# A gated attention and expert mix on one core: the spread of reciprocals, the layout of logit operands, a relu and the planner's clock are changed

## The chip, the cores and the metric

The kernel runs on one core of a Trainium2 chip. The metric is the device time of one execution in microseconds (us), smaller is better. Five engines work beside each other, each through its own list of instructions in order: PE (matrix products into the PSUM banks), DVE (vector work), ACT (activations), POOL (general vector work), and SP, which here issues every transfer. Transfers run on 16 DMA engines.

## The reference

A sequence of 2048 tokens of width 640 goes through an attention with 32 heads of width 20, in 4 segments of 512 tokens, with a memory carried from segment to segment. Beside it one token, the one with the largest router score, goes through a feed-forward expert. A gate mixes the two.

```python
phi = lambda t: where(t > 0, t + 1.0, exp(t))
for s in range(4):                                   # segments of 512 tokens
    logits = einsum("bhqd,bhkd->bhqk", qs, ks) * scale + mask
    a_dot  = softmax(logits) @ vs
    a_mem  = (phi(qs) @ M) / (phi(qs) . z + 1e-6)
    o      = g * a_mem + (1 - g) * a_dot             # g: sigmoid(beta), one per head
    M, z   = M + phi(ks)^T vs, z + sum(phi(ks))
a = concat(o) @ wo
b = x, plus sigmoid(r) * SwiGLU(x[i]) at the token i with the largest r = x @ w_r
out = sigmoid(x . gate_w) * a + (1 - sigmoid(x . gate_w)) * b
```

## The kernel before

The work is cut into 8 units (2 halves of 16 heads x 4 segments) and each unit into 4 groups of 4 heads, 32 groups in all; a group is numbered n, its unit u, its place in the unit g, its segment s.

For each unit PE makes the projections (`t_job` for q and k, transposed, in five tiles of 128 rows; `v_job` for v), in three products of split halves (a value is kept as a high part hi and a rest lo, made by `split`: ACT casts, DVE or POOL subtracts). Both run in `paired`, which uses the two row halves of PE at once. A product tile is evacuated by `evac_t`: DVE copies PSUM to `xs`, hi and lo are stored to DRAM by `place`, and phi is made as POOL min with 0 (L671), ACT exp (L672), DVE max (L673). A tile holds pieces of several groups (`TILES`), so `place` stores each piece by itself into an array of its group and kind, `stk`: three blocks of 80 rows, hi, hi, lo for q and hi, lo, hi for k.

For each group `fetch` loads q and k from these arrays as 60 rows x 2 halves x 2 column pairs. `a_step` (six per group) makes logits once only for their row maxima, which DVE takes (L785); `maxima` turns them, and two small transfers add them to q as rows (`qs<-mr`). `b_step` (six) makes the logits again with the maxima subtracted, ACT takes exp (L826), POOL sets the masked half to 0 (L828). `pv_step` multiplies with v, whose extra column of ones gives the sums; DVE copies the result to `pvs` (L851). For s > 0 `memory_read` makes the memory's part `num` and its denominators.

`norm` then divides. The denominators of the four heads, one row each, are collected (`zr<-pvs`, and `zr<-num` before it) into 128 x 16, inverted and gated on DVE, stored to DRAM as rows (`zrow<-zr`), and read back spread over all head rows, `rb<-zrow`: four blocks, each repeated 32 times, 2 KB a row for s = 0 and 4 KB for s > 0. DVE multiplies `pvs` (L872), POOL `num` (L875), DVE adds (L876), and the result goes to `oT` in DRAM, from which `o_load` and `o_job` make the output rows.

The order is written by a planner while the kernel is built. `Plan.add` notes every instruction with a duration, a key (about the number of the group at which it is due) and its buffers; `Plan.order` then plays the engines forward: each engine takes, of the instructions that could start earliest, the one with the lowest key. The transfer clock, the durations (`acts`, `dves`, `pools`) and the keys set the order in which each engine finds its instructions; on the chip that order is fixed, and an engine whose next instruction must wait, waits. All transfers stand in SP's list (`dma`, L376). The lines of the transfer clock before:

```python
count, size = t.desc
busy = max(count * (0.008 + size / 23400.0) / 16.0, 0.03)
dma_free = max(dma_free, t.fin + 0.9) + busy
t.fin = dma_free + 0.9
```

`t.fin` ahead of these lines is the end of the issue, 0.42 us (`ISSUE`) after its start.

Of the kernel before, what the change touches and what calls it, by code (L numbers as in the profile page):

```python
# [9 lines left out]
F32 = mybir.dt.float32  # L10
# [40 lines left out]
LEAD = 3.2  # L51
KPARTS = tuple((g, c0) for rows in TILES for _, _, kind, g, c0 in rows if kind == "k")
# [51 lines left out]
class Plan:  # L104
# [3 lines left out]
    ISSUE = 0.42  # L108
# [64 lines left out]
    def order(self):  # L173
# [22 lines left out]
        def choose(e):  # L196
# [50 lines left out]

        while len(done) < total:
# [85 lines left out]
def tile_infini_mod(  # L334
# [40 lines left out]
    def dma(key, dst, src, reads, writes, desc):  # L375
        plan.add("SP", Plan.ISSUE, lambda: nc.sync.dma_start(dst, src), key, reads, writes, desc=desc)  # L376

# [12 lines left out]
    def acts(n):  # L390
        return 0.2 + n / 1250.0
# [4 lines left out]
    def pools(n):  # L396
        return 0.12 + n / 460.0
# [4 lines left out]
    def split(key, engine, hi, lo, src, n, reads, hpart, lpart):  # L402

        act(key, acts(n), lambda: nc.scalar.copy(hi, src), reads, [hpart])  # L404
        e, dur = (nc.gpsimd, pools(n)) if engine == "POOL" else (nc.vector, dves(n))
        plan.add(engine, dur, lambda: e.tensor_tensor(out=lo, in0=src, in1=f32(hi), op=OP.subtract), key,  # L406
                 [*reads, hpart], [lpart])
# [52 lines left out]
    def constants():  # L460
# [10 lines left out]
        for i in range(4):  # L471
            pool(-4.6 + 0.1 * i, 1.2, lambda t=k_ring.tiles[i]: nc.gpsimd.memset(f32(t), 1.0), [], [kones[i]])
        for i in range(2):
            pool(-4.0, 0.2, lambda t=mneg[i].t: nc.gpsimd.memset(f32(t), 0.0), [], [(mneg[i], p) for p in "zhl"])
# [93 lines left out]
    def paired(ps, steps, operands, n, key_of, reads_of, kind):  # L568

        total, last, phase = len(steps), None, steps[0][1]  # L570
        for i, (k, ph) in enumerate(steps):
# [17 lines left out]
            last = pe(key_of(i), 3 * stream(n) + 0.01, fn, reads_of(k), [ps], opens=ps if i == 0 else None, fence=fence)  # L589
# [65 lines left out]
    def evac_t(u, j, ps, b, key):  # L655
# [11 lines left out]
        for r0, r1, kind, g, c0 in TILES[j]:  # L667
            place(kind, 4 * u + g, c0, hi, lo, r0, r1 - r0, key)
        if s < SEG - 1 or (s > 0 and j != 2):
            e = phi_ring.take()  # L670
            pool(key + 0.2, pools(L), lambda: nc.gpsimd.tensor_scalar(e.t, xs.t, 0.0, None, op0=OP.min), [xs], [e])  # L671
            act(key + 0.2, acts(L), lambda: nc.scalar.activation(e.t, e.t, AF.Exp), [e], [e])  # L672
# [25 lines left out]
    def memory_read(u, g, key):  # L698
# [13 lines left out]
        dma(key, z.t[:, 1, :], rows4(nb.t), [nb], [(z, 1)], (128, 64))  # L712
        pool(key, 0.15, lambda: nc.gpsimd.tensor_scalar(z.t[:, 1, :], z.t[:, 1, :], 1e-6, None, op0=OP.add), [(z, 1)], [(z, 1)])
# [47 lines left out]
    def a_step(n, p, t, key):  # L761
# [22 lines left out]
        for i, at_, w in blocks:  # L784
            dve(key - 0.6, 0.09 + 2 * w / 960.0, lambda i=i, at_=at_, w=w: nc.vector.tensor_reduce(  # L785
                out=m_.t[:, :, p, i], in_=banks[ps.pair][:, :, at_:at_ + w], axis=AX.X, op=OP.max), [ps], [(m_, (p, i))])

    def maxima(n, key):
# [65 lines left out]
    def norm(n, o, key):  # L854
# [17 lines left out]
        dve(key, dves(L), lambda: nc.vector.tensor_tensor(out=o.t, in0=o.t, in1=rb.t[:, 0, :], op=OP.mult), [o, rb], [o])  # L872
        if s:
            nb = nums.pop(n)
            pool(key, pools(L), lambda: nc.gpsimd.tensor_tensor(out=nb.t, in0=nb.t, in1=rb.t[:, 1, :], op=OP.mult), [nb, rb], [nb])  # L875
            dve(key, dves(L), lambda: nc.vector.tensor_tensor(out=o.t, in0=o.t, in1=nb.t, op=OP.add), [o, nb], [o])  # L876
# [26 lines left out]
    def route():  # L903
# [28 lines left out]
        plan.add("SP", 1.2, load, key, [ix], [xr], desc=(128, 20))  # L932
# [96 lines left out]
    def o_load(s, k, key):  # L1029
# [3 lines left out]
        while r < 128:  # L1033
# [11 lines left out]
            dma(key - 0.5, b.t[r:r + cnt, :L], src, [oTb[n] for n in reads], [(b, r)], (cnt, 2048))  # L1045
# [3 lines left out]
    def o_job(s, t, key, span):  # L1049
# [5 lines left out]
        act(key - 0.2, acts(D), lambda: nc.scalar.activation(xf, xf, AF.Copy, scale=R["gb"].t[:, i:i + 1]), [xb, R["gb"]], [xb])  # L1055
        dve(key - 0.2, dves(D), lambda: nc.vector.scalar_tensor_tensor(
# [10 lines left out]
        dve(key + span, dves(D), lambda: nc.vector.scalar_tensor_tensor(  # L1067
# [109 lines left out]
```

## Time and profile before

| | |
|---|---|
| time, median of 3 runs | 918.67 us (915.0 to 923.78) |
| profiled execution: its own time | 923.43 us |
| profiled execution: span, first to last instruction | 921.7 us |
| mean granted clock of PE | 0.841 |
| busy: PE, DVE, ACT, POOL | 654.5, 438.8, 309.8, 370.2 us |
| transfers on SP's queue | 77296 packets, 133.89 MB, 50.4% of the 16 engines' span |

The profile is of one execution. A group of instructions is one source line on one engine with its tiles (out<-in), with the number of instructions, their busy time, the mean of one in ns, and the idle time of the engine just before them with what ended it. The chain is the work that ended last, followed back from the end. In the timeline each row has start, duration, engine, line, tiles, and in brackets the idle time before it. In the table of stretches each row has the stretch, its length, the busy times of PE, PE's weight loads, DVE, ACT and POOL, then PE's granted clock, the share of the DMA engines in use, and GB/s.

### The profile page before, as it was taken

The page shows a single profiled execution, that of the slowest core. Times are in us where ns is not written, and L with a number is a line of the kernel's source. Part 1 is how long each engine was busy: PE and PEld are TensorE (multiplying, and loading weights), DVE is VectorE, ACT ScalarE, POOL GpSimd, SP SyncE. Part 2 cuts the span into 40 slices and gives each one's busy share as a digit, 9 for nine tenths or more (in the row PEclk, how much of TensorE's full clock was granted, in tenths as well). Part 3 has the DMA queues.
Part 4 walks back from the last instruction along what each step waited for, and adds up shares of the span by engine and source line. Part 5 has one row for each costly group of instructions (what it writes and reads, how often), then busy time and mean ns, then how long its engine had stood idle before and what let it go on. Part 6 is the DMA issues. An engine that isn't in the chain of part 4 may idle for free.

```text
span 921.7 us, 19377 instructions
## 1 busy us (share of the span) xinstructions
PE 654.5 (71%) x7760; PEld 486.4 (53%) x7760; DVE 438.8 (48%) x771; ACT 309.8 (34%) x536; POOL 370.2 (40%) x446
## 2 busy tenths in 40 slices
PE   5778778766788763675778679756775956568667
PEld 3675566445545541354556466544444734356567
DVE  8537445643544554444356345533563544443323
ACT  5234345233333342531424325322332324133210
POOL 8735325443433542363334325442443426151310
PEclk9889899779779975876989879977888977779879
DMA  7754562445325544256437664666446753334531
GB/s 232 217 158 127 142 195 85 135 140 154 90 83 158 160 107 118 77 159 196 137 101 208 170 182 126 202 176 176 126 130 187 229 140 128 116 113 137 146 129 73
DMA packets 77386, 135.12 MB, mean 147 GB/s; under 512 B 24338, under 2 KB 27952, under 8 KB 77296
## 3 DMA queue, kind: packets, MB, share of 16 engines
q1 hardware_dynamic: 77296, 133.89, 50.4%
q8 instruction: 61, 1.00, 0.5%
q14 instruction: 29, 0.24, 0.1%
HBM read 87.30 MB, written 45.56 MB: 144 GB/s over the span
## 4 chain that ended last, share of the span: by engine, by line
DMA 39%; PE 27%; DVE 11%; issue 9%; SPq 6%; POOL 5%; ACT 3%; ACTq 0%; POOLq 0%; DVEq 0%
DMA rb<-zrow 15%; PE bank L587 14%; DMA zrow<-zr 6%; SPq L376 6%; PE bank L847 4%; DVE mx L785 3%; DMA qs<-mr 3%; PE bank L821 2%; DMA zr<-pvs 2%; PE bank L773 2%; DMA raw<-in_wc_dram 2%; POOL num L875 2%; DMA out_dram<-xf 2%; PE bank L706 1%; DMA xf<-in_x_dram 1%
## 5 line engine op out<-in xcount | busy, mean ns | idle before, releaser
L785 DVE TENSOR_REDUCE mx<-bank 128x2 f32<-128x1024 f32 (+3 forms) x256 | 199.6, 816 | 54.8 <-PE bank L779 44.9
L773 PE MATMUL bank<-ks,qs 60*128 60x512 f32 (+3 forms) x512 | 93.0, 398 | 64.5 <-DVE mx L785 34.2
L587 PE MATMUL bank<-xhi,whi 64*128 64x512 f32 (+1 forms) x480 | 102.6, 407 | 33.9 <-ACT whi L404 22.9
L875 POOL TENSOR_TENSOR num<-num,rb 128x512 f32<-128x512 f32 x24 | 42.4, 1766 | 170.4 <-DMA rb<-zrow 170.4
L826 ACT ACTIVATE pb<-bank 128x768 f32<-128x768 f32 x128 | 101.1, 816 | 28.2 <-PE bank L821 22.8
L826 ACT ACTIVATE pa<-bank 128x1024 f32<-128x1024 f32 x64 | 65.7, 1027 | 126.9 <-PE bank L821 120.1
L872 DVE TENSOR_TENSOR pvs<-pvs,rb 128x512 f32<-128x512 f32 x32 | 24.3, 758 | 174.1 <-DMA rb<-zrow 174.1
L821 PE MATMUL bank<-qs,ks 62*128 62x512 f32 (+3 forms) x512 | 81.5, 366 | 34.8 <-DMA qs<-mr 19.2
L773 PEld LDWEIGHTS bank<-ks,qs 60*128 60x128 f32 x512 | 54.7, 214 | 83.2 <-DVE mx L785 39.6
L587 PE MATMUL bank<-xhi,wlo 64*128 64x512 f32 (+1 forms) x480 | 96.0, 381 | 3.4 <-DVE wlo L406 2.2
L587 PE MATMUL bank<-xlo,whi 64*128 64x512 f32 (+1 forms) x480 | 95.2, 378 | 0.5 <-POOL xlo L406 0.3
L828 POOL TENSOR_SCALAR_AFFINE_SELECT pb<-pb 128x256 f32<-128x256 f32 (+1 forms) x128 | 73.9, 584 | 42.5 <-ACT pb L826 40.0
L828 POOL TENSOR_SCALAR_AFFINE_SELECT pa<-pa 128x256 f32<-128x256 f32 x64 | 29.6, 463 | 140.6 <-ACT pa L826 139.2
L821 PEld LDWEIGHTS bank<-qs,ks 62*128 62x128 f32 x512 | 51.8, 199 | 54.8 <-issue 10.8
L406 POOL TENSOR_TENSOR xlo<-raw,xhi 128x512 fp32r<-128x512 f32 x53 | 68.4, 1308 | 22.9 <-ACT xhi L404 22.3
L587 PEld LDWEIGHTS bank<-xhi,whi 64*128 64x128 f32 x480 | 53.5, 205 | 44.1 <-ACT whi L404 23.1
L587 PE MATMUL bank<-whi,xhi 64*128 64x320 f32 x320 | 54.8, 338 | 23.0 <-DVE nil L575 19.1
L587 PE MATMUL bank<-vhi,xhi 64*128 64x322 f32 x320 | 64.5, 375 | 6.1 <-DVE nil L575 6.1
L671 POOL TENSOR_SCALAR phi<-xs 128x512 f32<-128x512 f32 x38 | 57.0, 1499 | 23.7 <-DVE xs L664 11.0
L709 ACT COPY num<-bank 128x512 f32<-128x512 f32 x24 | 14.1, 585 | 155.5 <-DVE pvs L851 42.8
L847 PE MATMUL bank<-pb,va 128*32 128x128 f32 (+2 forms) x768 | 56.7, 422 | 5.8 <-POOL pb L828 5.8
L587 PE MATMUL bank<-vlo,xhi 64*128 64x322 f32 x320 | 58.8, 341 | 0.0
(126 smaller groups left out, 1346.8 us busy)
## 6 DMA issues: line engine op xcount, KB each, us to landing
qs<-stkq SPq DMA_DIRECT2D x64, 240.0 KB
ks<-stkk SPq DMA_DIRECT2D x64, 240.0 KB
rb<-zrow SPq DMA_DIRECT2D x24, 512.0 KB
stkq<-hi SPq DMA_DIRECT2D x32, 320.0 KB
raw<-in_xT_dram SPq DMA_DIRECT2D x35, 256.0 KB
oT<-pvs SPq DMA_DIRECT2D x32, 256.0 KB
stkq<-lo SPq DMA_DIRECT2D x32, 160.0 KB
raw<-in_wg_dram SPq DMA_DIRECT2D x15, 288.0 KB
```

The costliest lines, as they stand in the source:

```text
L376: plan.add("SP", Plan.ISSUE, lambda: nc.sync.dma_start(dst, src), key, reads, writes, desc=desc)
L406: plan.add(engine, dur, lambda: e.tensor_tensor(out=lo, in0=src, in1=f32(hi), op=OP.subtract), key, [*reads, hpart], [lpart])
L587: nc.tensor.matmul(t[:, b, :n], w[64 * r:64 * r + 64], m[64 * r:64 * r + 64], start=i == 0 and p == 0, stop=ends and p == 2, skip_group_ch ...
L671: pool(key + 0.2, pools(L), lambda: nc.gpsimd.tensor_scalar(e.t, xs.t, 0.0, None, op0=OP.min), [xs], [e])
L773: nc.tensor.matmul(a[:, b, at_:at_ + w], q.t[64 * b:64 * b + ST, p, 128 * i:128 * i + 128], k.t[64 * b:64 * b + ST, p, :w], start=m == 0, ...
L785: dve(key - 0.6, 0.09 + 2 * w / 960.0, lambda i=i, at_=at_, w=w: nc.vector.tensor_reduce(out=m_.t[:, :, p, i], in_=banks[ps.pair][:, :, at ...
L821: nc.tensor.matmul(bt[:, b, at_:at_ + w], k.t[64 * b:64 * b + ST + 2, p, 128 * c:128 * c + 128], q.t[64 * b:64 * b + ST + 2, p, L - w:], s ...
L826: act(key - 0.4, 0.22 + 2 * w / 1270.0, lambda: nc.scalar.activation(pt.t, banks[ps.pair][:, :, :w], AF.Exp, scale=SCALE), [ps], [pt])
L828: pool(key, 0.42 if t < 2 else 0.64, lambda: nc.gpsimd.affine_select(out=d, in_=d, pattern=[[0, 2], [0, len(cs)], [1, 128]], base=0, chann ...
L847: nc.tensor.matmul(o[32 * j:32 * j + 32, ps.bank, L - w:], v.t[:, c, VW * h:VW * h + 32], pt[j % 2, min(c, 2)].t[:, j // 2, at_:at_ + w], ...
L872: dve(key, dves(L), lambda: nc.vector.tensor_tensor(out=o.t, in0=o.t, in1=rb.t[:, 0, :], op=OP.mult), [o, rb], [o])
L875: pool(key, pools(L), lambda: nc.gpsimd.tensor_tensor(out=nb.t, in0=nb.t, in1=rb.t[:, 1, :], op=OP.mult), [nb, rb], [nb])
```

## The change

- `norm`: the spread of reciprocals is read in four transfers of 20 rows, one per head, in place of one of 128 rows. The 12 rows between heads are set to 1 once, by two memsets on POOL at the start.
- `stk` is one array per unit, three blocks of 640 rows (hi, hi, lo). `place` stores a whole tile: hi twice in one transfer, lo in another. `fetch` picks 20 rows from each of the three blocks, q from the first on, k from the last back, and waits for the tiles that hold its rows.
- phi: POOL's min with 0 goes. ACT makes relu(-x), then exp of its negative; DVE's part stays.
- The transfer clock: 0.65 us from issue to the first byte, packets on as many engines as the transfer is said to use (`wide`: 16, or 10 for `fetch` and the spread), 0.3 us to the end. `ISSUE` is 0.36, with durations of their own for several transfers; several durations of engine work are changed.
- PE's choice: the keys of projection steps are 1.2 later. A step that opens a bank for `a_step` (read by DVE) or `b_step` (read by ACT) loses rank when the work already waiting for that engine reaches more than 0.5 us past the step's end.

```diff
+LATER = 1.2
+PATIENCE = 0.5
+SHY = 2.0
+DRAIN = {"a": "DVE", "b": "ACT"}
+ROWS = {(kind, g): (min(128 * j + r0 for j, rows in enumerate(TILES) for r0, _, k_, g_, _ in rows if (k_, g_) == (kind, g)),
+                    [j for j, rows in enumerate(TILES) for _, _, k_, g_, _ in rows if (k_, g_) == (kind, g)])
+        for kind in "qk" for g in range(4)}
...
-    ISSUE = 0.42
+    ISSUE = 0.36
...
+                late = {}
+                for x in ("ACT", "DVE"):
+                    late[x] = free[x] + sum(t.dur for t in avail[x] if not t.gone)
+
+                def rank(c):
+                    est, t = c
+                    k = t.key
+                    if t.opens is not None and t.opens.kind in DRAIN:
+                        x = late[DRAIN[t.opens.kind]] - (est + t.dur + 0.3) - PATIENCE
+                        if x > 0:
+                            k += SHY * x
+                    return k, t.seq
+                return min(now, key=rank)
...
-                count, size = t.desc
-                busy = max(count * (0.008 + size / 23400.0) / 16.0, 0.03)
-                dma_free = max(dma_free, t.fin + 0.9) + busy
-                t.fin = dma_free + 0.9
+                count, size, wide = t.desc
+                each = 0.008 + size / 23400.0
+                begin = max(dma_free, t.fin + 0.65)
+                dma_free = begin + count * each / 16.0
+                t.fin = max(dma_free, begin + -(-count // wide) * each) + 0.3
...
     def pools(n):
-        return 0.12 + n / 460.0
+        return 0.17 + n / 455.0
...
-    stk = {kind: [Buf(dram.tile([3 * GC, L], F32, name=f"stk{kind}{n}")) for n in range(NG)] for kind in "qk"}
+    stk = [Buf(dram.tile([3 * D, L], F32, name=f"stk{u}")) for u in range(NU)]
...
+        for i in range(2):
+            pool(-1.0, 1.0, lambda t=rb_ring.tiles[i]: nc.gpsimd.memset(t, 1.0), [], [rones[i]])
...
-            last = pe(key_of(i), 3 * stream(n) + 0.01, fn, reads_of(k), [ps], opens=ps if i == 0 else None, fence=fence)
+            last = pe(key_of(i) + (LATER if kind != "O" else 0.0), 3 * stream(n) + 0.01, fn, reads_of(k), [ps], opens=ps if i == 0 else None, fence=fence)
...
-    def place(kind, n, c0, hi, lo, r0, cnt, key):
-        d = stk[kind][n]
-        first, gap, low = {"q": (0, GC, 2 * GC), "k": (0, 2 * GC, GC)}[kind]
-        src = f32(hi.t)[r0:r0 + cnt, :]
-        dma(key, bass.AP(tensor=d.t.tensor, offset=d.t.offset + (first + c0) * L, ap=[[L, cnt], [gap * L, 2], [1, L]]),
+    def place(u, j, hi, lo, key):
+        d = stk[u]
+        src = f32(hi.t)[:, :]
+        dma(key, bass.AP(tensor=d.t.tensor, offset=d.t.offset + 128 * j * L, ap=[[L, 128], [D * L, 2], [1, L]]),
...
-            [hi], [(d, (c0, "h"))], (2 * cnt, 2048))
-        dma(key, d.t[low + c0:low + c0 + cnt, :], f32(lo.t)[r0:r0 + cnt, :], [lo], [(d, (c0, "l"))], (cnt, 2048))
+            [hi], [(d, (j, "h"))], (256, 2048))
+        dma(key, d.t[2 * D + 128 * j:2 * D + 128 * j + 128, :], f32(lo.t)[:, :], [lo], [(d, (j, "l"))], (128, 2048))
...
-        for r0, r1, kind, g, c0 in TILES[j]:
-            place(kind, 4 * u + g, c0, hi, lo, r0, r1 - r0, key)
+        place(u, j, hi, lo, key)
...
-            pool(key + 0.2, pools(L), lambda: nc.gpsimd.tensor_scalar(e.t, xs.t, 0.0, None, op0=OP.min), [xs], [e])
-            act(key + 0.2, acts(L), lambda: nc.scalar.activation(e.t, e.t, AF.Exp), [e], [e])
+            act(key + 0.2, acts(L), lambda: nc.scalar.activation(e.t, xs.t, AF.Relu, scale=-1.0), [xs], [e])
+            act(key + 0.2, acts(L), lambda: nc.scalar.activation(e.t, e.t, AF.Exp, scale=-1.0), [e], [e])
...
-            d = stk[kind][n]
+            r0, js = ROWS[kind, g]
+            first, step = (r0, D * L) if kind == "q" else (2 * D + r0, -D * L)
...
-                dma(key, dst.rearrange("r p t -> r (p t)"), bass.AP(tensor=d.t.tensor, offset=d.t.offset + 2 * b * L,
-                                                                    ap=[[4 * L, ST], [1, 2 * L]]), [d], [(b_, b)], (ST, 4096))
+                dma(key, dst.rearrange("r p t -> r (p t)"), bass.AP(tensor=d.t.tensor, offset=d.t.offset + (first + 2 * b) * L,
+                                                                    ap=[[4 * L, DH], [step, 3], [1, 2 * L]]),
+                    [(d, (j, a)) for j in js for a in "hl"], [(b_, b)], (ST, 4096), 10)
...
-        dma(key, sub(rb.t, 0, [[1, L * i]]), bass.AP(tensor=d.t.tensor, offset=d.t.offset, ap=[[2 * L, 4], [0, 32], [1, L * i]]),
-            [d], [rb], (128, 2048 * i))
+        for j in range(4):
+            dma(key, rb.t[32 * j:32 * j + DH, :i, :].rearrange("p i t -> p (i t)"),
+                bass.AP(tensor=d.t.tensor, offset=d.t.offset + 2 * L * j, ap=[[0, DH], [1, L * i]]), [d], [(rb, j)],
+                (DH, 2048 * i), 10)
```

The remaining lines change durations alone: for instance 0.58 for the issue of `zr<-num`, 0.6 for `zr<-pvs`, 0.56 for `zrow<-zr`, 0.68 for `qs<-mr`, 1.75 for POOL's product with `rb`, 0.89 for the sum behind it, 0.06 more for a maximum, and 0.07 to 0.4 more for some others.

More of the change, by code (lines that the diff above doesn't have):

```diff
@@ L373, in tile_infini_mod, with dma @@
     banks = [psum.tile([128, 2, 512], F32, name=f"bank{i}") for i in range(PAIRS)]
-    def dma(key, dst, src, reads, writes, desc):
-        plan.add("SP", Plan.ISSUE, lambda: nc.sync.dma_start(dst, src), key, reads, writes, desc=desc)
+    def dma(key, dst, src, reads, writes, desc, wide=16, issue=Plan.ISSUE):
+        plan.add("SP", issue, lambda: nc.sync.dma_start(dst, src), key, reads, writes, desc=(*desc, wide))
     def dve(key, dur, fn, reads, writes):
@@ L396, in pools, with split @@
     def pools(n):
-        return 0.12 + n / 460.0
+        return 0.17 + n / 455.0
     def stream(n):
         return max(n * 0.000447 + 0.003, 0.11)
-    def split(key, engine, hi, lo, src, n, reads, hpart, lpart):
-        act(key, acts(n), lambda: nc.scalar.copy(hi, src), reads, [hpart])
-        e, dur = (nc.gpsimd, pools(n)) if engine == "POOL" else (nc.vector, dves(n))
+    def split(key, engine, hi, lo, src, n, reads, hpart, lpart, more=0.0):
+        act(key, acts(n) + 0.4 * more, lambda: nc.scalar.copy(hi, src), reads, [hpart])
+        e, dur = (nc.gpsimd, pools(n) + 0.4 * more) if engine == "POOL" else (nc.vector, dves(n) + more)
         plan.add(engine, dur, lambda: e.tensor_tensor(out=lo, in0=src, in1=f32(hi), op=OP.subtract), key,
@@ L452, in tile_infini_mod @@
     oTb = [Buf(oT) for _ in range(NG)]
-    stk = {kind: [Buf(dram.tile([3 * GC, L], F32, name=f"stk{kind}{n}")) for n in range(NG)] for kind in "qk"}
+    stk = [Buf(dram.tile([3 * D, L], F32, name=f"stk{u}")) for u in range(NU)]
     zrow = [Buf(dram.tile([4, 2, L], F32, name=f"zrow{n}")) for n in range(NG)]
+    rones = [Buf(t) for t in rb_ring.tiles]
+    rb_ring.last = list(rones)
     kones = [Buf(t) for t in k_ring.tiles]
@@ L505, in w_split @@
             split(key, engine, sub(whi[k].t, at_, dd), sub(wlo[k].t, at_, dd), sub(raw, from_, sd), 2 * GC, reads,
-                  (whi[k], p), (wlo[k], p))
+                  (whi[k], p), (wlo[k], p), 0.4)
     def v_split(hf, qq, k, raw, reads, key, engine):
@@ L711, in memory_read @@
         zr[n] = z = zr_ring.take()
-        dma(key, z.t[:, 1, :], rows4(nb.t), [nb], [(z, 1)], (128, 64))
-        pool(key, 0.15, lambda: nc.gpsimd.tensor_scalar(z.t[:, 1, :], z.t[:, 1, :], 1e-6, None, op0=OP.add), [(z, 1)], [(z, 1)])
+        dma(key, z.t[:, 1, :], rows4(nb.t), [nb], [(z, 1)], (128, 64), issue=0.58)
+        pool(key, 0.26, lambda: nc.gpsimd.tensor_scalar(z.t[:, 1, :], z.t[:, 1, :], 1e-6, None, op0=OP.add), [(z, 1)], [(z, 1)])
     def rows4(t):
@@ L808, in maxima @@
             dma(key, f32(q.t)[64 * b + ST:64 * b + ST + 2].rearrange("r p (i t) -> r (p i) t", t=128),
-                mr.t[16 * b:16 * b + 16], [mr], [(q, ("m", b))], (16, 512))
+                mr.t[16 * b:16 * b + 16], [mr], [(q, ("m", b))], (16, 512), issue=0.68)
     def b_step(n, p, t, key):
@@ L858, in norm @@
         i = 2 if s else 1
-        dma(key, z.t[:, 0, :], rows4(o.t), [o], [(z, 0)], (128, 64))
+        dma(key, z.t[:, 0, :], rows4(o.t), [o], [(z, 0)], (128, 64), issue=0.6)
         zz = z.t[:, :i, :]
         ps_ = [(z, a) for a in range(i)]
-        dve(key, 0.3, lambda: nc.vector.reciprocal(zz, zz), ps_, ps_)
+        dve(key, 0.35, lambda: nc.vector.reciprocal(zz, zz), ps_, ps_)
         dve(key, 0.22, lambda: nc.vector.tensor_tensor(out=zz, in0=zz, in1=sub(gts.t, 2 * (4 * hf + g), [[1, i], [0, 16]]),
@@ L874, in norm @@
             nb = nums.pop(n)
-            pool(key, pools(L), lambda: nc.gpsimd.tensor_tensor(out=nb.t, in0=nb.t, in1=rb.t[:, 1, :], op=OP.mult), [nb, rb], [nb])
-            dve(key, dves(L), lambda: nc.vector.tensor_tensor(out=o.t, in0=o.t, in1=nb.t, op=OP.add), [o, nb], [o])
+            pool(key, 1.75, lambda: nc.gpsimd.tensor_tensor(out=nb.t, in0=nb.t, in1=rb.t[:, 1, :], op=OP.mult), [nb, rb], [nb])
+            dve(key, 0.89, lambda: nc.vector.tensor_tensor(out=o.t, in0=o.t, in1=nb.t, op=OP.add), [o, nb], [o])
         h = HH * hf + 4 * g
@@ L931, in load @@
             nc.sync.dma_start(xr.t, x[bass.ds(i, 1), :].rearrange("o (p t) -> (o p) t", t=KT))
-        plan.add("SP", 1.2, load, key, [ix], [xr], desc=(128, 20))
+        plan.add("SP", 1.2, load, key, [ix], [xr], desc=(128, 20, 16))
         R.update(gx=gx, gb=gb, oh=oh, sg=sg, xr=xr)
@@ L1044, in o_load @@
             reads = sorted({16 * (h_ // HH) + 4 * s + h_ % HH // 4 for h_ in hs})
-            dma(key - 0.5, b.t[r:r + cnt, :L], src, [oTb[n] for n in reads], [(b, r)], (cnt, 2048))
+            dma(key - 0.5, b.t[r:r + cnt, :L], src, [oTb[n] for n in reads], [(b, r)], (cnt, 2048), issue=0.77 if cnt > 20 else 0.46)
             r += cnt
@@ L1066, in o_job @@
                lambda k: [*X[NU + s, k], *((w[k], p) for w in (whi, wlo) for p in WALL)], "O")
-        dve(key + span, dves(D), lambda: nc.vector.scalar_tensor_tensor(
+        dve(key + span, dves(D) + 0.07, lambda: nc.vector.scalar_tensor_tensor(
             out=sub(xf, 0, [[320, 2], [1, 320]]), in0=banks[ps.pair][:, :, :320], scalar=R["gx"].t[:, i:i + 1],
```

10 lines of the change are left out of this document (6 added, 4 removed).

## The prediction, made before the changed kernel ran

> **What bounds the kernel now.** I read the page first, then the waits, then stretches of the timeline, and last the busy times inside the stretches that the waits named.
>
> ```profile
> span 921.7 us, 19377 instructions
> ...
> PE 654.5 (71%) x7760; PEld 486.4 (53%) x7760; DVE 438.8 (48%) x771; ACT 309.8 (34%) x536; POOL 370.2 (40%) x446
> ...
> DMA 39%; PE 27%; DVE 11%; issue 9%; SPq 6%; POOL 5%; ACT 3%; ACTq 0%; POOLq 0%; DVEq 0%
> DMA rb<-zrow 15%; PE bank L587 14%; DMA zrow<-zr 6%; SPq L376 6%; PE bank L847 4%; DVE mx L785 3%; DMA qs<-mr 3%; PE bank L821 2%; DMA zr<-pvs 2%; PE bank L773 2%; DMA raw<-in_wc_dram 2%; POOL num L875 2%; DMA out_dram<-xf 2%; PE bank L706 1%; DMA xf<-in_x_dram 1%
> ...
> L671 POOL TENSOR_SCALAR phi<-xs 128x512 f32<-128x512 f32 x38 | 57.0, 1499 | 23.7 <-DVE xs L664 11.0
> ...
> L872 DVE TENSOR_TENSOR pvs<-pvs,rb 128x512 f32<-128x512 f32 x32 | 24.3, 758 | 174.1 <-DMA rb<-zrow 174.1
> ```
>
> No engine is full: the busiest, PE, works 71% of the span. The chain is made of transfers, and its largest line is rb, the reciprocals spread over the head rows. The waits say who stands still for it:
>
> ```profile
> DVE pvs L872 <- DMA rb<-zrow: 174.1, 30, 10.2
> POOL num L875 <- DMA rb<-zrow: 170.4, 24, 14.5
> ...
> ACT phi L672 <- POOL phi L671: 42.1, 16, 10.8
> ...
> PE bank L821 <- DMA qs<-mr: 19.2, 8, 6.6
> ```
>
> Engines take their instructions in the planner's order, so a DVE that waits at L872 also holds back the maxima, the evacuations and the phase copies queued behind. One such stall, from the timeline of SP, DVE and POOL:
>
> ```profile
> 320.40 0.56 SPq L376 DMA_DIRECT2D rb<-zrow  x1
> ...
> 322.03 1.40 SPq L376 DMA_DIRECT2D qs<-mr  x2
> ```
> ```profile
> 328.62 0.69 DVE L872 TENSOR_TENSOR pvs<-pvs,rb 128x512 f32<-128x512 f32 x1 [7.84 <-DMA rb<-zrow]
> ```
> ```profile
> 328.67 1.77 POOL L875 TENSOR_TENSOR num<-num,rb 128x512 f32<-128x512 f32 x1 [10.11 <-DMA rb<-zrow]
> ```
>
> Next, busy times by stretch: 5 us inside that stall, 2.4 us of another transfer of rb, and the sum row over the 30 stretches in which DVE waits at L872 (PE is the second figure).
>
> ```profile
> 323.00:328.00 5.00, 0.00 (x0) 0.00 (x0) 0.00 (x0) 0.18 (x1) 0.00 (x0) 0.70 0.27 98
> 190.80:193.20 2.40, 1.57 (x26) 1.02 (x22) 1.14 (x2) 2.23 (x5) 1.49 (x1) 1.00 0.24 99
> ```
> ```profile
> sum 174.16, PE 74.87 PEld 43.23 DVE 0.12 ACT 36.05 POOL 23.63; mean PE 2.50 PEld 1.44 DVE 0.00 ACT 1.20 POOL 0.79
> ```
>
> Two readings. From 323 to 328 us PE does nothing: the whole core waits for rb. And meanwhile the transfers fill only 0.24 to 0.27 of the 16 DMA engines, 98 to 99 GB/s: about four engines at 25 GB/s each. The source of rb is four blocks, each repeated 32 times, and four is what is busy.
>
> **rb in four transfers, and its clock.** The chain of waits has the hops of the normalisation:
>
> ```profile
> 82.33 4.65 DMA rb<-zrow
> ...
> 236.53 1.95 DMA zrow<-zr
> 238.53 10.05 DMA rb<-zrow
> ...
> 261.41 1.98 DMA qs<-mr
> ...
> 322.03 7.32 DMA qs<-mr
> ...
> 871.00 11.68 DMA rb<-zrow
> ```
>
> A hop of 8 KB takes 1.95 us from issue to landing. Before, 128 rows of 4 KB are 512 KB, 5.2 us at 99 GB/s, so rb needs about 7.2 us alone, and with company 8.2 (320.40 to 328.62) to 11.7; 256 KB, in units without a memory read, took 4.65. The planner's clock says 0.42 + 0.9 + 1.46 + 0.9 = 3.7 us. It puts L872 too early by the difference, and the mean stall, 174.1/32 = 5.4 us, is what that makes.
>
> After: 20 rows per transfer, 80 in all, 320 KB. Price of an issue and of neighbours (SP durations min/median/max):
>
> ```profile
> L376 SPq DMA_DIRECT2D qs<-stkq x64: 315/404/2034, 30.2 to 738.2; - x64
> ```
> ```profile
> 208.50:211.50 3.00, 3.00 (x54) 3.00 (x52) 1.29 (x4) 1.16 (x2) 1.45 (x3) 1.00 0.86 239
> ```
>
> Three more issues of 0.40 and a gap of 0.04 put the last one 1.3 us behind the first. No transfer of 20 rows with one repeated row is in this trace. If each still keeps four engines busy the 320 KB take 3.3 us; if they fill 16 at 25 GB/s, 0.8. The 60-row fetches, second row, fill 0.86 of the engines, so outermost sizes above four do spread; I take 1.6 us, most of it beside the four issues. Landing: 1.3 + 1.95 + about 0.3 = 3.5 us after the first issue (3.2 to 5.5). The new clock plans 4 x 0.36 + 0.65 + 0.37 + 0.3 = 2.8. What stays is 0.7 us of error, plus the 0.9 by which today's stall exceeds today's error (5.4 against 8.2 - 3.7 = 4.5), plus something for the clock of the small hops, which becomes 1.6 us against the measured 1.95 where it was 2.3: I take 1.8 us per group, 58 us in all (42 to 100). Removed: 174 - 58 = 116 us of stall. What is queued behind rb on SP, such as the copies of the maxima at 322.03, goes out 1.3 us later, but no longer waits behind 5 us of data.
>
> The Trainium skill, DMA: Bandwidth & Descriptors, section "Why a DMA increments its semaphore by 16 and not by 1", says that a transfer issued from SP uses the largest number of engines up to 16 that divides the outermost size on both sides, and always the lowest-numbered ones. The 0.24 to 0.27 agree with four engines for rb; by the rule 20 rows use 10, the data then take 1.3 us as an estimate, and the sum would be 4 us lower. The same rule speaks against the change in one place: by it the fetches go from 60 rows outermost (15 engines) to 20 (10).
>
> What a removed microsecond is worth: inside the stalls PE is busy 74.87/174.16 = 0.43, outside (654.5 - 74.9)/(921.7 - 174.2) = 0.775. The work done inside a stall must still be done, at the outside pace, so 1 us less stall saves 1 - 0.43/0.775 = 0.445 us. 116 x 0.445 = **52 us**.
>
> Two smaller parts of rb.
>
> ```profile
> 882.70 0.69 DVE L872 TENSOR_TENSOR pvs<-pvs,rb 128x512 f32<-128x512 f32 x1 [3.32 <-DMA rb<-zrow]
> ```
>
> The two copies of the maxima (qs<-mr) are issued right behind rb and land after 7.32 instead of 1.98 us; PE waits 19.2 us in all for them. Half of that lies inside the stalls already counted; **5 us**. At the end, rb of the last group takes 11.68 us on the chain while only 3.3 of it is a DVE stall; about 6 more go, less what the loads of oT beside it keep: **5 us**.
>
> **Relu on ScalarE.**
>
> ```profile
> L671 POOL TENSOR_SCALAR phi<-xs x38: 1478/1488/1921, 23.4 to 726.1; 128x512 f32<-128x512 f32 x38
> L672 ACT ACTIVATE phi<-phi x38: 627/632/679, 24.9 to 732.3; 128x512 f32<-128x512 f32 x38
> ```
>
> POOL loses 38 x 1.5 = 57 us, ACT gains 38 x 0.63 = 24 (34% to 36% busy); phi comes 0.86 us earlier and without a change of engine. The new instruction waits for xs, as the cast of hi ahead of it on ACT does already, so nothing new is held. ACT's 42.1 us of waiting for POOL go, off the path mostly: **3 us** gained (from 10 gained to 8 lost if the softmax exponentials get late behind it).
>
> **One array per unit.**
>
> ```profile
> L376 SPq DMA_DIRECT2D stkq<-hi x32: 322/426/1443, 23.9 to 729.8; - x32
> L376 SPq DMA_DIRECT2D stkq<-lo x32: 303/417/1562, 27.1 to 731.9; - x32
> ...
> L376 SPq DMA_DIRECT2D stkk<-hi x64: 316/482/1740, 24.3 to 728.5; - x64
> L376 SPq DMA_DIRECT2D stkk<-lo x64: 302/438/1729, 28.1 to 731.0; - x64
> ```
> ```profile
> 235.92 1.17 SPq L376 DMA_DIRECT2D zrow<-zr  x2
> ```
> ```profile
> L472 POOL MEMSET ks<- 128x1024 f32 x4 | 3.9, 1019 | 0.0
> ```
>
> 24 stores per unit become 10: 8 x 14 x 0.45 = 50 us less issuing on SP, of which 96 more issues of rb take 38 back. The bytes stay. SP is 6% of the chain, so I count 0 (3 gained at most). The new clock books a fetch on 10 engines (its last argument) instead of 16; I charge nothing, since ten at the 25 GB/s of rb give the 239 to 250 GB/s that the row at 208.50 shows already; where that fails, a fetch takes half as long again, under a lead of two groups. A fetch also waits for a whole tile, not its piece: the same bytes in fewer issues, 0. That fetches of one group and stores of the next tile lie in one array could bring false waits, but two zrow stores with interleaved rows go out back to back, in 1.17 us, so addresses are told apart. Two memsets of rb, as large as these of ks, cost POOL 2 us in the start-up; I count **1 us** lost.
>
> **The order.** LATER, the rank of a- and b-banks and the other durations only move instructions. No row prices a new order; I take 0, with 30 gained and 85 lost (below) as ends.
>
> Sum: 52 + 5 + 5 + 3 - 1 = 64, so 65 in round numbers. The profiled execution took 923.4 us (span 921.7), 4.8 above the median of the three runs, 918.7. Against it 858; in medians **854 us**.
>
> **Rivals.**
>
> *The new order loses.* LATER puts every projection step 1.2 groups behind in PE's choice, so the next unit's operands come late.
>
> ```profile
> 82.33 0.56 SPq L376 DMA_DIRECT2D rb<-zrow  x1
> ...
> 871.00 0.58 SPq L376 DMA_DIRECT2D rb<-zrow  x1
> ```
> ```profile
> 172.58 0.68 DVE L664 COPY xs<-bank 128x512 f32<-128x512 f32 x1
> ```
> ```profile
> 190.71 0.48 PE L773 MATMUL bank<-ks,qs 60*128 60x512 f32 x2
> ```
> ```profile
> 216.07 0.34 PE L773 MATMUL bank<-ks,qs 60*128 60x256 f32 x4
> ```
> ```profile
> 234.94 0.68 PE L821 MATMUL bank<-qs,ks 62*128 62x512 f32 x4
> ```
>
> A group lasts (871.0 - 82.3)/31 = 25.4 us, so 1.2 groups are 30. At the start of unit 2 the second tile is evacuated at 172.6 and its first logits start at 190.7, the storing and fetching between; the second pass starts 18.5 us after the first has ended. Cover is therefore some 18 us, and the loss 12 us at each of 7 starts, 85 in all: 918.7 - 65 + 85 = 939. It decides only where PE has always something nearer to do; PE idles 29% of the span and takes what is ready, which speaks against it. Chance 0.08.
>
> *The four transfers queue on the same four engines.* 320 KB then take 3.3 us, landing at 5 to 6.4, and (5.7 - 2.8 + 0.9) x 32 = 122 us of stall stay: 52 x 0.445 + 12 = 35 gained, 884. The Trainium skill, DMA: Bandwidth & Descriptors, "Rules for kernel authors", advises against splitting by partitions, as the parts serialize on the same engines; it assumes a transfer that fills all 16, which the 0.24 denies here. Chance 0.08.
>
> *Another wait takes its place.* PE then stands behind DVE's maxima or the small hops, whose planned time is now too short; half the 52 comes back: 880 to 910, say 890. Chance 0.12.
>
> *The order gains too.* All 174 us go and 25 more: 815. Chance 0.10.
>
> My forecast has 0.62, about 830 to 880. A measurement here tells 1% from no change. Faster by over 1%: 0.87; within: 0.05; slower: 0.08. The range from 815 to 905 leaves out the slow rival and the tails of the others.
>
> **What would show it.** DVE's wait for rb at L872 near 60 us, POOL's at L875 likewise; rb landing 3.5 us after its first issue; DMA share during it well above 0.25; qs<-mr at 2 to 3 us; L671's group gone from POOL, and ACT at about 335 us busy with one table load still; 80 stores into the arrays where there were 192, 128 transfers of rb where there were 32. I am wrong if those waits fall and the idle time of PE (267 us) does not, or if logits at the start of a unit wait for their fetch.

## The result, and the profile after

The changed kernel takes 813.19 us in the median of 4 runs (808.57 to 816.36), the kernel before 917.97 beside it: a ratio of 0.8848, interval 0.8786 to 0.8910. That is 105 us less; the forecast was 65, and the time lies just under the lower end of the range. The profiled execution took 816.36 us, span 814.6. Its page, and what waits for rb (`L903` is the old L872, `L906` the old L875):

```profile
span 814.6 us, 19424 instructions
...
PE 650.7 (80%) x7760; PEld 488.9 (60%) x7760; DVE 431.2 (53%) x775; ACT 337.0 (41%) x574; POOL 313.2 (38%) x410
...
DMA 36%; PE 29%; DVE 11%; SPq 7%; issue 6%; ACT 5%; POOL 5%; DVEq 0%; ACTq 0%; POOLq 0%
PE bank L613 16%; SPq L398 7%; DMA rb<-zrow 6%; DMA zrow<-zr 5%; PE bank L876 4%; DVE mx L814 4%; DMA zr<-pvs 3%; DMA xf<-in_x_dram 3%; PE bank L850 3%; DMA out_dram<-xf 2%; DMA qs<-mr 2%; DMA stk<-lo 2%; DMA rrow<-best 2%; PE bank L802 2%; DMA raw<-in_wg_dram 2%
```
```profile
POOL num L906 <- DMA rb<-zrow: 85.4, 18, 16.5
DVE pvs L903 <- DMA rb<-zrow: 80.2, 26, 6.7
...
PE bank L850 <- DMA qs<-mr: 14.6, 12, 2.4
```

rb falls from 15% to 6% of the chain, DVE's wait for it from 174.1 to 80.2 us, POOL's from 170.4 to 85.4. PE is busy nearly as long as before (650.7 us against 654.5); its idle time falls from 267 to 164 us, which is nearly the whole gain. One spread, from SP and DVE, and a stretch inside it:

```profile
174.80 1.42 SPq L398 DMA_DIRECT2D rb<-zrow  x4
```
```profile
179.21 0.69 DVE L903 TENSOR_TENSOR pvs<-pvs,rb 128x512 f32<-128x512 f32 x1 [4.06 <-DMA rb<-zrow]
```
```profile
176.50:177.50 1.00, 0.66 (x18) 0.26 (x8) 0.00 (x0) 0.00 (x0) 0.00 (x0) 1.00 0.47 57
```

4.4 us from the first issue to DVE's start, where the shown stall of before took 8.2, and 0.47 of the DMA engines in use where it was 0.24 to 0.27. In the median over the stalls of each trace it is 4.8 us (26 stalls), before 9.0 (29).

### The profile page after: what moved, and what is told of

Same layout as the page of the kernel before. It is cut to its first block, busy times and chain, and to the rows that moved or that the text cites. A ratio compares the mean times of both kernels' runs of the same rounds, so it can differ in the third digit from the quotient of the medians.

```text
span 814.6 us, 19424 instructions
## 1 busy us (share of the span) xinstructions
PE 650.7 (80%) x7760; PEld 488.9 (60%) x7760; DVE 431.2 (53%) x775; ACT 337.0 (41%) x574; POOL 313.2 (38%) x410
## 4 chain that ended last, share of the span: by engine, by line
DMA 36%; PE 29%; DVE 11%; SPq 7%; issue 6%; ACT 5%; POOL 5%; DVEq 0%; ACTq 0%; POOLq 0%
PE bank L613 16%; SPq L398 7%; DMA rb<-zrow 6%; DMA zrow<-zr 5%; PE bank L876 4%; DVE mx L814 4%; DMA zr<-pvs 3%; DMA xf<-in_x_dram 3%; PE bank L850 3%; DMA out_dram<-xf 2%; DMA qs<-mr 2%; DMA stk<-lo 2%; DMA rrow<-best 2%; PE bank L802 2%; DMA raw<-in_wg_dram 2%
## 5 line engine op out<-in xcount | busy, mean ns | idle before, releaser
L613 PE MATMUL bank<-xhi,whi 64*128 64x512 f32 (+1 forms) x480 | 113.8, 433 | 9.8 <-ACT whi L426 6.2
L850 PE MATMUL bank<-qs,ks 62*128 62x512 f32 (+3 forms) x512 | 88.8, 377 | 30.7 <-DMA qs<-mr 14.6
L613 PE MATMUL bank<-xhi,wlo 64*128 64x512 f32 (+1 forms) x480 | 104.4, 395 | 1.1 <-DVE wlo L428 0.9
L613 PE MATMUL bank<-xlo,whi 64*128 64x512 f32 (+1 forms) x480 | 103.2, 391 | 0.0
L802 PEld LDWEIGHTS bank<-ks,qs 60*128 60x128 f32 x512 | 60.2, 212 | 69.9 <-DVE mx L814 18.5
L428 POOL TENSOR_TENSOR xlo<-raw,xhi 128x512 fp32r<-128x512 f32 x53 | 69.2, 1326 | 52.1 <-ACT xhi L426 51.7
L850 PEld LDWEIGHTS bank<-qs,ks 62*128 62x128 f32 x512 | 55.8, 203 | 49.3 <-DVE mx L814 10.4
L906 POOL TENSOR_TENSOR num<-num,rb 128x512 f32<-128x512 f32 x24 | 41.2, 1718 | 104.6 <-DMA rb<-zrow 85.4
L613 PEld LDWEIGHTS bank<-xhi,whi 64*128 64x128 f32 x480 | 59.0, 214 | 19.0 <-ACT whi L426 6.2
L903 DVE TENSOR_TENSOR pvs<-pvs,rb 128x512 f32<-128x512 f32 x32 | 23.9, 748 | 80.3 <-DMA rb<-zrow 80.2
L428 POOL TENSOR_TENSOR lo<-xs,hi 128x512 fp32r<-128x512 f32 x40 | 52.7, 1333 | 30.6 <-ACT hi L426 30.2
L613 PEld LDWEIGHTS bank<-xhi,wlo 64*128 64x128 f32 x480 | 59.1, 213 | 6.1 <-DVE wlo L428 2.4
L613 PEld LDWEIGHTS bank<-xlo,whi 64*128 64x128 f32 x480 | 58.6, 212 | 6.7 <-POOL xlo L428 0.4
```

The costliest lines, as they stand in the source:

```text
L613: nc.tensor.matmul(t[:, b, :n], w[64 * r:64 * r + 64], m[64 * r:64 * r + 64], start=i == 0 and p == 0, stop=ends and p == 2, skip_group_ch ...
L802: nc.tensor.matmul(a[:, b, at_:at_ + w], q.t[64 * b:64 * b + ST, p, 128 * i:128 * i + 128], k.t[64 * b:64 * b + ST, p, :w], start=m == 0, ...
L850: nc.tensor.matmul(bt[:, b, at_:at_ + w], k.t[64 * b:64 * b + ST + 2, p, 128 * c:128 * c + 128], q.t[64 * b:64 * b + ST + 2, p, L - w:], s ...
L906: pool(key, 1.75, lambda: nc.gpsimd.tensor_tensor(out=nb.t, in0=nb.t, in1=rb.t[:, 1, :], op=OP.mult), [nb, rb], [nb])
```

## The experiments

All ratios are to the kernel before, run beside it on the same chip. On these chips the kernel before took 914 to 918 us, so a difference in microseconds between two experiments is good to a few microseconds. Waits and busy times come from one profiled execution. A kernel that keeps an order unchanged issues every other instruction of every engine in the same sequence as the kernel it is made from.

**e1: the spread alone.** On the kernel before (what stands in < > is put in words):

```diff
-        dma(key, sub(rb.t, 0, ...), <4 blocks, each 32 times>, [d], [rb], (128, 2048 * i))
+        def spread():
+            for j in range(4):
+                nc.sync.dma_start(<20 rows of head j>, <its row, 20 times>)
+        plan.add("SP", Plan.ISSUE, spread, key, [d], [rb], desc=(128, 2048 * i))
```

> The kernel before with its order unchanged; only the spread of reciprocals is issued as four transfers of 20 rows at the place of the one (and the rb buffers are set to 1 at the start). Theory A (the stall at the spread is the main loss, a microsecond less of it is worth 0.445): DVE's wait for rb falls from 174 to about 35 us and the time to about 850. Theory B (a microsecond of that stall is worth about one, since everything behind it is late): below 800 to 815, the whole gain of the change. Theory C (the new order brings most of the gain): above 890.

807.69 us, ratio 0.8807 (0.8758 to 0.8856): the whole gain, with no instruction of the other engines moved. (Two memsets of rb are added on POOL at the start.)

```profile
span 816.5 us, 19569 instructions
...
PE 643.8 (79%) x7760; PEld 482.7 (59%) x7760; DVE 438.8 (54%) x771; ACT 310.0 (38%) x536; POOL 370.1 (45%) x448
```
```profile
POOL num L882 <- DMA rb<-zrow: 58.7, 17, 10.2
DVE pvs L879 <- DMA rb<-zrow: 57.2, 19, 6.4
```

DVE's wait falls by 116.9 us and the time by 110: 0.94 us per microsecond of stall, not 0.445. The profiled execution of e1 is some 10 us above its median; from the spans of the profiled executions, 921.7 and 816.5, the price is 0.90. POOL's wait falls with DVE's here, by 112 us, so this is the price of both together.

**e2: the change without it.** The changed kernel, order unchanged; the fourth transfer is replaced by the old one of 128 rows, the first three go.

> The changed kernel with its order unchanged; the spread goes out as one transfer of 128 rows where the fourth stood. Theory A: the order counts on 2.8 us, the transfer lands after 8 to 9, DVE's wait for rb rises from 80 to about 210 us and the time by 0.445 x 130 to about 870. Theory B: 930 or more, slower than the kernel before, because this order counts on the short transfer. Theory C: below 835.

933.05 us, ratio 1.0181 (1.0121 to 1.0241): nothing of the gain is left, and the time is 1.8% above the kernel before.

```profile
POOL num L908 <- DMA rb<-zrow: 211.0, 23, 23.0
DVE pvs L905 <- DMA rb<-zrow: 205.2, 32, 12.4
```

Against the changed kernel DVE's wait rises by 125 us, the time by 120: 0.96, and 0.94 from the spans (814.6 and 932.0). The order was planned for the short transfer, so this does not say what the rest of the change would do in an order planned for the long one.

**e4: the stall taken away by the order alone.** The kernel before, with its transfer clock told that rb lands later:

```diff
-                t.fin = dma_free + 0.9
+                t.fin = dma_free + 0.9 + sum(more)      # rb: 4.7 for s > 0, else 1.7
```

> The kernel before with only the planned landing of the spread set to what the trace shows (4.7 us later for 4 KB rows, 1.7 for 2 KB), so that the multiplications by it stand later in the order. If the loss is the misplaced instruction and not the length of the transfer: DVE's wait for rb falls below 60 us and the time to 850 to 870 without any change of transfers. If the length itself is on the path: the wait goes to other places and the time stays above 895.

864.74 us, ratio 0.9443 (0.9399 to 0.9486).

```profile
PE bank L821 <- DMA qs<-mr: 50.1, 22, 6.6
...
DVE pvs L872 <- DMA rb<-zrow: 43.8, 15, 5.6
```

DVE's wait falls by 130 us, more than in e1, but the time by 53 only, 0.41 per microsecond, and PE's wait for the copies of the maxima rises from 19.2 to 50.1. Half of the gain comes without any change of a transfer. That those copies wait behind the long transfer on its engines may be part of it, but was not tried by itself, and it cannot be all: in the changed kernel, without the long transfer, such copies on the chain take up to 6.8 us too.

**e7 and e18: engines or bytes.** e1, with the source of each transfer written so that its outermost size is 4 (e7), and with 32 rows a transfer (e18), which moves the 512 KB of before:

```diff
-    ap=[[0, DH], [1, L * i]]
+    ap=[[0, 4], [0, DH // 4], [1, L * i]]      # e7
+    ap=[[0, 32], [1, L * i]]                   # e18, rows 32 * j to 32 * j + 32
```

> Run e1 with the same four transfers, rows, bytes and order, but the source written as 4 x 5 repeats in place of 20, so that the outermost size is four. If the number of engines is what the split buys: 0.25 of the engines busy during the spread, 3.3 us of data, DVE's wait for rb about 60 us more than in e1 (57 us) and the time 850 to 870. If the smaller bytes or the split itself do it: 803 to 822.

> Run e1 (808 us) with its order; each of the four transfers writes 32 rows in place of 20, so the bytes are those of the kernel before (512 KB for 4 KB rows) and the outermost size is 32. If the number of engines decides: 800 to 820 and DVE's wait for rb within 20 us of e1's 57. If the bytes do: most of the gain lost, 850 or more.

e7: 859.74 us, ratio 0.9399 (0.9352 to 0.9447). e18: 822.67 us, ratio 0.8931 (0.8860 to 0.9002). The SP rows are of e1 and of e7, the wait is of e7:

```profile
L876 SPq DMA_DIRECT2D rb<-zrow x128: 272/323/1277, 84.1 to 769.1; - x128
```
```profile
L876 SPq DMA_DIRECT2D rb<-zrow x128: 589/614/687, 80.9 to 811.0; - x128
```
```profile
DVE pvs L879 <- DMA rb<-zrow: 99.3, 28, 7.2
```

With the bytes of before the gain stays, but for some 12 to 15 us; with outermost size 4 half of it goes. But the transfers of e7 also take 0.29 us more each to issue, 37 us of SP over the run, which could by itself be most of the 42 us by which DVE's wait rises. The traces part the two. In the median over the stalls, the time from the first issue to DVE's start is 4.2 us in e1 and 6.6 in e7; the issues take 1.4 and 2.6 of it, and what follows the last issue 2.8 and 4.0. So about half of e7's delay is issuing, and half is data that take longer. In e18 what follows is 2.7 us, as short as in e1, with 1.6 times the bytes. So the outermost size counts, and the smaller volume hardly does.

**e9 and e10: what a microsecond costs, by itself.** e1, order unchanged, with work that changes no result put behind the sum on DVE (e9) or behind the product on POOL (e10), in the 24 groups with a memory read:

```diff
+    for _ in range(4): nc.vector.tensor_tensor(out=rb.t[:, 0, :], in0=rb.t[:, 0, :], in1=rb.t[:, 0, :], op=OP.max)   # e9
+    for _ in range(2): nc.gpsimd.tensor_scalar(rb.t[:, 1, :], rb.t[:, 1, :], 1.0, None, op0=OP.mult)                 # e10
```

> Run e1 (808 us) with its order unchanged and four more VectorE instructions of 0.69 us (a maximum of rb with itself, in place) behind the sum in each of the 24 groups with a memory read: 66 us of DVE time at the place of the stall, nothing else late. My price of 0.445: 29 us more, 837. If a microsecond of DVE there costs about one: 65 to 75 more, 870 to 885. If DVE has slack and the stall costs by POOL or by the transfer itself: below 823.

> Run e1 (808 us) with its order unchanged and two more GpSimd instructions of 1.5 us (rb times one, in place) behind the product with rb in each of the same 24 groups: 72 us of POOL time at the place of its stall. If POOL's stall has a share in the price: 20 us or more on top, 830 to 880. If only DVE's counts: 800 to 820.

e9: 870.22 us, ratio 0.9501 (0.9463 to 0.9539). e10: 840.57 us, ratio 0.9177 (0.9120 to 0.9234). Busy times and DVE's wait of e9, then busy times of e10:

```profile
span 867.1 us, 19664 instructions
...
PE 647.1 (75%) x7760; PEld 486.2 (56%) x7760; DVE 522.5 (60%) x867; ACT 310.6 (36%) x536; POOL 379.6 (44%) x448
...
DVE pvs L879 <- DMA rb<-zrow: 36.9, 15, 4.2
```
```profile
PE 650.5 (77%) x7760; PEld 487.2 (58%) x7760; DVE 435.0 (52%) x771; ACT 309.9 (37%) x536; POOL 442.8 (53%) x496
```

In e9 DVE is busy 83.7 us longer (522.5 - 438.8) and waits 20.3 us less for rb, so it is held 63.4 us more; the time rises by 62.5, or by 50.6 from the spans (816.5 and 867.1): 0.80 to 0.99, though DVE is busy only 60% of the span. This is DVE alone, without POOL and the transfer. In e10 POOL is busy 72.7 us longer and waits 7.0 us less for rb (51.7), so it is held 66 us more; the time rises by 33, half of that (24 from the spans).

**e3, e5, e6, e13: choice and clock.** e3 is the changed kernel with `LATER = 0` and `SHY = 0`; e5 the changed kernel with the four old lines of the transfer clock, but the new durations; e6 is e1 with the new choice; e13 is e6 with the relu and the arrays, its durations the old ones.

> The changed kernel with the old choice on TensorE: projection keys not delayed, no rank by the reader's backlog; new durations and transfer clock kept. My prediction's step (the order counts nothing): 805 to 825. Theory C: 850 to 870, the 40 us that the prediction missed.

> The changed kernel, its transfer clock alone set back to the formula before (0.9 us to start, 0.9 to land, all transfers of the list one after the other); the new choice and durations stay. Theory D (the new clock plans the hops too short, so that waiting instructions stand too early; that cost is what the new choice gains, and the two cancel): the wait for rb falls below 60 us and the time to 765 to 795. Theory E (the clock is neutral, something else in the change costs 50 us): 800 to 825.

> The kernel before with the spread in four transfers (run e1, 808 us) and the new choice on TensorE (projection keys 1.2 later, rank by the reader's backlog); old clock, durations, arrays and phi. Theory D: the choice gains here too, 755 to 785. If the choice only repairs what the new clock spoils: 800 to 820.

> Run e1 with the new choice, the relu and the arrays, but the transfer clock and all durations of before. If the choice only repairs what the new clock spoils (e6: no gain): 798 to 812, the sum of e6 and e8. If the choice gains once GpSimd is relieved: 775 to 795, as e5.

| | us | ratio (interval) |
|---|---|---|
| the change | 813.19 | 0.8848 (0.8786 to 0.8910) |
| e3: the change, old choice | 865.55 | 0.9451 (0.9404 to 0.9497) |
| e5: the change, old clock | 786.10 | 0.8594 (0.8564 to 0.8625) |
| e1: the spread alone | 807.69 | 0.8807 (0.8758 to 0.8856) |
| e6: e1 and the new choice | 810.13 | 0.8891 (0.8846 to 0.8936) |
| e13: e6, relu and arrays | 802.15 | 0.8774 (0.8716 to 0.8832) |

DVE's wait in e3, then in e5:

```profile
DVE pvs L903 <- DMA rb<-zrow: 135.2, 30, 10.6
```
```profile
DVE pvs L902 <- DMA rb<-zrow: 55.2, 23, 6.3
```

Beside all the rest of the change the new clock costs 27 us (e5). The new choice gains 52 beside the new clock (e3), and nothing beside the old clock with the old durations (e6 against e1): there it repairs, and adds nothing by itself. e5 is 16 us faster than e13, which differs from it mainly in the planned durations, so these gain something too. With the old choice DVE's wait for rb is 55 us longer and the time 52; that fits the price of e9, but the order differs, and e6 shows that with another order a shorter wait need not pay: DVE waits 37.5 us there, 57.2 in e1, and the times are equal.

**e8 and e11: relu, arrays, fetches.** e8 is e1 with the relu and the arrays; e11 is e1, order unchanged, with each fetch's source written as 20 x 3 rows in place of 60.

> Run e1 (808 us) with the relu on ScalarE and one array per unit added; clock, durations and choice of before. My prediction: 3 us gained by the relu, nothing by the arrays, 797 to 812 with the order that the planner makes of it. Theory E (the arrays, with fetches on 10 engines that wait for whole tiles, or the relu, cost what the choice gains): 840 to 865.

> Run e1 (808 us) with its order, rows and bytes unchanged; the source of each fetch is written as 20 x 3 rows in place of 60, the outermost size of the changed kernel. My prediction's step (nothing, the fetches have a lead): 800 to 818. If a fetch on fewer engines holds up logits or the transfers behind it: 825 or more.

e8: 805.34 us, ratio 0.8808 (0.8762 to 0.8854), the same as e1. e11: 816.08 us, ratio 0.8896 (0.8858 to 0.8934), 8 us above e1, at the edge of what these intervals tell apart.

**e12, e14 to e17: the length of the planned hops.** The changed kernel with other latencies in its clock, nothing else:

```diff
-                begin = max(dma_free, t.fin + 0.65)
+                begin = max(dma_free, t.fin + A)
...
-                t.fin = max(dma_free, begin + -(-count // wide) * each) + 0.3
+                t.fin = max(dma_free, begin + -(-count // wide) * each) + B
```

> The changed kernel, new clock kept in form, with 0.8 us to the first byte in place of 0.65 and 0.6 us to the end in place of 0.3, so that a hop of 8 KB is planned at about the measured 1.95 us. If the 27 us that the new clock costs come from hops planned too short: 770 to 797. If they come from its form (transfers may overlap in the plan, where the old one puts them in a row): 805 to 820.

> The changed kernel with its clock's two latencies at 0.9 and 0.9 us, as long as the old clock's 1.8 in all, but in the new form. If the length of the planned hops decides (0.95: 813, 1.4: 806): 780 to 795, as e5 with the old form. If the form decides: 800 to 815.

> The same with 1.3 and 1.3 us, 2.6 in all, 1.2 us more than a hop of 8 KB takes after its issue. If every wait avoided counts and later places cost nothing: DVE's wait for rb below 30 us and 765 to 785. If instructions that stand too late cost as much as waits: 795 or more.

> The changed kernel with 1.8 and 1.8 us in its clock, 3.6 in all. If waits avoided are all that counts: DVE's wait for rb below 20 us, 755 to 770. If late places begin to cost (the chain of hops of each group is planned over 10 us long, buffers stay taken): 773 to 795.

> The same with 2.6 and 2.6 us, 5.2 in all. By the first theory no wait is left and the time stays at that of e16; by the second it is clearly above e15, 790 to 830.

| A + B, us | us | ratio (interval) | DVE's wait for rb, us |
|---|---|---|---|
| 0.65 + 0.3 (the change) | 813.19 | 0.8848 (0.8786 to 0.8910) | 80.2 |
| 0.8 + 0.6 (e12) | 806.48 | 0.8825 (0.8772 to 0.8879) | 76.9 |
| 0.9 + 0.9 (e14) | 794.16 | 0.8675 (0.8599 to 0.8750) | 55.5 |
| 1.3 + 1.3 (e15) | 773.01 | 0.8427 (0.8363 to 0.8492) | 34.3 |
| 1.8 + 1.8 (e16) | 727.26 | 0.7948 (0.7898 to 0.7998) | 31.7 |
| 2.6 + 2.6 (e17) | 749.48 | 0.8222 (0.8165 to 0.8278) | 17.5 |

e16, its busy times, and its wait at the spread:

```profile
PE 616.9 (85%) x7760; PEld 464.4 (64%) x7760; DVE 437.0 (60%) x772; ACT 334.4 (46%) x574; POOL 317.0 (44%) x410
```
```profile
DVE pvs L903 <- DMA rb<-zrow: 31.7, 15, 5.2
```

e12 gained little, which by its expectation spoke for the form of the clock; e14, in the same form with the old clock's 1.8 us, came within 8 us of e5, so most of the 27 us lie in the length. e16 and e17 fell outside what either theory expected.

The shortest hops of 8 KB take 1.95 us, 1.4 after the issue of 0.56; planning all of them there is not the best, for others take longer. The chain of the changed kernel, which picks late ones, has 14 hops of `zrow`, from 1.9 to 6.0 us and 2.9 in the mean; three of them, with start and duration:

```profile
78.60 1.96 DMA zrow<-zr
...
170.07 4.65 DMA zrow<-zr
...
285.77 5.97 DMA zrow<-zr
```

e16 plans 3.6 us and beats both kernels, by 86 us the changed one. e17 has the shortest wait for rb and is slower than e16, so places that are too late seem to cost too. From e15 to e16 DVE's wait falls by 3 us only and the time by 46. By the two profiles, PE's busy time falls by 22 us (from 638.9) for the same 7760 matrix products, with its granted clock at 0.902 and then 0.923, and its idle time by 28, from 136 to 108. Which waits those 28 us were stays open, and each value is one order only, so single steps of this table may be luck of that order. That all first five fall in time as they grow in length is hardly luck.

## Why the prediction was wrong in size

**The reading of the bound was right.** rb was the main loss, it lay on about four engines, and taking it apart removed it; e1 shows it alone, e2 shows its absence.

**The stall removed was sized somewhat too large.** Foreseen were 116 us; the change removes 93.9 (174.1 to 80.2), leaving 80.2 where I took 58, inside my 42 to 100. The 116.9 of e1 is near 116 by chance: e1 keeps the old clock, and for it I expected 139 (174 to 35). Landing was taken at 3.5 us (3.2 to 5.5); the median is 4.8.

**The step that failed is the price, 0.445 us for a microsecond of stall.** Measured with the order unchanged by e1, e2 and e9: 0.94, 0.96 and 0.99, or 0.90, 0.94 and 0.80 from the spans of the profiled executions. With the stall that the change really removed, 93.9 us, the old price gives 42 us and 0.94 gives 88; with the 12 of the small parts that is 100 of the 105 measured. I had set PE's pace inside the stalls against its pace everywhere else, 0.775, and that pace was itself pulled down by the stalls. The trace of before shows it. The two rows are sums over the 30 stalls: the 4 us behind each, then the 8 us behind those (PE is the second figure), lengths chosen after the result:

```profile
sum 120.00, PE 54.84 PEld 38.47 DVE 98.36 ACT 19.34 POOL 89.00; mean PE 1.83 PEld 1.28 DVE 3.28 ACT 0.64 POOL 2.97
```
```profile
sum 240.00, PE 210.42 PEld 155.51 DVE 143.74 ACT 70.11 POOL 77.19; mean PE 7.01 PEld 5.18 DVE 4.79 ACT 2.34 POOL 2.57
```

When rb has landed DVE works through what it held back, 98 of 120 us busy, and PE goes on waiting: 0.46 busy, where the pace behind that is 210.42/240 = 0.877. Counted so, the stalls and the 4 us behind them are 294 us in which PE did 129.7 us of work, worth 148 at that pace: 146 us lost for 174 of stall, 0.84.

PE's granted clock belongs in the count too. Over the same stretches its mean is 0.84 in the stalls, 0.65 in the 4 us behind them and 0.78 in the next 8, where by difference the rest of the span has about 0.94. So a busy microsecond behind a stall does less work: with each stretch's busy time weighted by its clock, the stalls and the 4 us behind them lose 163 us against the pace of the rest, which is 0.94 per microsecond of stall (an estimate; 1.1 with the next 8 us). All of that stood in the trace that I had. That the pause lowers the clock is not shown; the low clock behind the stalls is.

The price holds for the order unchanged only. By e4 a microsecond of wait removed by the order alone was worth 0.41, close to my 0.445, but that is another case: there other waits took the stall's place.

**The order was put at nothing, and came out near nothing as a sum of larger terms.** Everything beside the spread and the new clock gains 22 us (e5 against e1), and the new clock loses 27; the whole rest of the change is 813 against 808 us. That the terms cancel is luck. Had I priced the clock, I would have seen the loss: I noted that it plans a small hop at 1.6 us against 1.95 measured, and charged it only in the 58 us. The rival "the new order loses" had the right object and the wrong part of it: delayed projections together with the new rank gain (e3; the delay alone was not tried), planning hops short loses. The rival "the order gains too" named 815 us, nearly the time measured, but not for its reasons: 80 of the 174 us of stall stayed, and the order gained nothing in sum.

**The small parts.** Relu and arrays: 3 us forecast, none measured (e8). POOL's work fell from 370.2 to 313.2 us and ACT's rose to 337.0, as worked out. Fetches: nothing forecast, 8 us at the edge of the intervals (e11). Copies of the maxima: PE's wait fell from 19.2 to 14.6 us, by 4.6 where I took half of it; they were to land in 2 to 3 us, and four of them on the chain take 3.3 to 6.8. The 5 us at the end were not measured by themselves. The rival in which the transfers stay on four engines was put at 884 us; e7, which writes them so but in the old order, took 860.

## What to carry to other kernels

When an engine works through a fixed order, a stall can cost its length and the time in which the others refill behind it: compare with the pace well behind a stall, and weigh busy time with the clock, rather than take the mean outside it. Put a term for the price of waiting to a test by itself (a few instructions of known length at that place, order unchanged) before anything is built on it. And a planner's latencies are not best at the time of the shortest hop: here 2.6 and 3.6 us beat 1.4, and 5.2 was slower than 3.6 again.

## What the runs showed of the hardware

How the source of a transfer is written can cost more than its bytes: 512 KB with outermost size 4 took 8 to 12 us at 0.24 to 0.27 of the 16 DMA engines, and the same bytes in four transfers with outermost size 32 kept nearly the whole gain (e18). The Trainium skill, DMA: Bandwidth & Descriptors, "Why a DMA increments its semaphore by 16 and not by 1", has the number of engines follow from the outermost sizes; the four engines of the trace agree with it. The same page of the Trainium skill, under "Rules for kernel authors", advises one transfer of 128 partitions rather than parts, on the ground that each part already uses all 16 engines; the source of before did not, and with four parts the kernel was 12% faster (e1).

The form of a transfer also sets what it costs to issue: 0.32 us for 20 repeats of one row, 0.61 for the same rows as 4 x 5 repeats (medians of e1 and e7).

Beside some work of POOL, work of DVE took longer. In e9 most of the added DVE maxima took 0.69 us, but some up to 1.77 (first row: minimum, median and maximum in ns; second: the group, with its mean):

```profile
L886 DVE TENSOR_TENSOR rb<-rb x96: 677/693/1774, 165.8 to 831.5; 128x512 f32<-128x512 f32 x96
```
```profile
L886 DVE TENSOR_TENSOR rb<-rb 128x512 f32<-128x512 f32 x96 | 91.4, 952 | 2.5
```

The timeline of e9 shows when: in the six groups where POOL ran nothing beside them, the four maxima took 2.85 to 2.87 us together; in the groups where POOL made a rest lo or its min with 0 beside them, 3.9 to 6.2.
